# Turning B by DMA, three half blocks first, one tile's statistics on ScalarE, one power for the root in the opening part of a fused layernorm, SSM and SwiGLU kernel

## Chip, cores, metric

One core of a Trainium2 chip. The metric is device time of the whole program in microseconds (us), median of several executions, compared with the kernel before on the same chip. The kernel before takes 190.64 us; its executions lie within 0.2%.

The engines are called as the profile does: PE is TensorE (matmul), PEld its weight loads, DVE VectorE, ACT ScalarE, POOL GpSimd, SP SyncE (here it mainly issues DMAs). A letter q behind a name is the engine's instruction queue. The granted clock is the share of its full clock that TensorE is given. L428 is line 428 of that kernel's source; the numbers shift between kernels.

## The reference, cut to what matters

```python
def _A_ref(x, ...):                       # SSM: x is 2048 tokens x 448
    Lam_bar = exp(exp(log_dt) * Lam)
    Bu = einsum("bld,pd->blp", x, B_bar)  # "bu": needs B turned, as matmul weights
    for t in range(L): h = Lam_bar * h + Bu[:, t]
    return 2.0 * einsum("blp,dp->bld", hseq, C).real + x * Dskip

def _B_ref(x, w_gate, w_up, w_down):      # 448 -> 1792 -> 448
    return (silu(x @ w_gate) * (x @ w_up)) @ w_down

x = A_x; xn = layernorm(x)                # mean, variance, 1/sqrt(v + 1e-5)
return x + A(xn) * silu(B(xn))
```

## The kernel before

The 2048 tokens are worked in four quarters of 512 (four tiles of 128 tokens). For a quarter, gate and up take 14 blocks of 128 columns, two at a time ("pairs" of blocks, four banks a pair, of the eight banks of PSUM, into which TensorE writes). ScalarE evicts them, that is, copies them out of PSUM so that the bank is free (`gs` by Silu, `us` by Copy), and VectorE multiplies four blocks in one instruction. The argument touches these parts (cuts marked by ...).

```python
def bank(name, dtype=F32):            # eight banks, handed out in turn
    return psum.tile([P, 2048 // mybir.dt.size(dtype)], dtype, name=name, tag="bank")
...
def gu(q, bg, budget, hooks={}, begun=None):
    ...
            for i in range(0, n, 2):
                fi = f0 + i
                ...
                    banks = gu_banks()
                    gu_matmuls(q, fi, banks, 0, W)
                for j, (gp_, up_) in enumerate(banks):
                    nc.scalar.activation(gs[:, i + j, :], gp_[:], ACT.Silu)
                    nc.scalar.activation(us[:, i + j, :], up_[:], ACT.Copy)
                for fn in hooks.get(fi // 2, ()):   # hook n runs after pair n
                    fn()
```

The matmuls use half the rows of the array each, two at a time. Where the halves change places, GpSimd passes a notice on to TensorE (`tell`: an empty instruction in GpSimd's stream), and powers run on GpSimd between such notices:

```python
def tell(mm):
    told = nc.gpsimd.nop(nofuse=True)
    ...
def ln_sqrt(n0, n1):  power(sd[:, n0:n1], vep[:, n0:n1], halves[:, 0 : n1 - n0])   # on GpSimd
def ln_rstd(n0, n1):  nc.vector.reciprocal(out=rstd[:, n0:n1], in_=sd[:, n0:n1])
```

The rest of the first quarter's work hangs in the hooks. `table_phase` is four VectorE instructions that make the arguments of a cos/sin table, `table_sin` two ScalarE instructions (ST, CT) that evaluate it; `bu` is the group of B's products:

```python
gu(0, bg, 2.0, {
    0: [*stats(4, 5, 6, 7), *sqrt(1), on(params_in), on(table_phase, 0)],
    1: [*bs(1), on(b_clear), *rstd_of(1), *norms(4, 5, 6, 7), on(table_sin, 0)],
    2: [*transposes(4, 5, 6, 7), on(load_c), on(table_phase, 1), on(table_sin, 1),
        on(bu, 0, (0, 1)), on(table_phase, 2), on(table_sin, 2)],
    3: [on(bu, 0, (2,), "between"), on(table_phase, 3), on(table_sin, 3), on(params_fold)],
    4: [on(params_trig), on(ssm_steps, bg, 0)],
    5: [on(params_out)],
}, begun)
```

In these traces ScalarE and VectorE run their instructions in the order of the program: what is written first on ScalarE runs first there, even where it waits (the 3.21 us of waiting before a table, shown below, hold the evictions behind it).

## Time and profile before

| what | value |
|---|---|
| time | 190.64 us |
| TensorE busy | 97% of 188.8 us |
| first gate/up matmul | 7.22 us |
| first `bu` matmul | 19.38 us |
| first matmul of the down projection | 64.3 us |
| last matmul ends | 184.7 us |

From TensorE's and VectorE's timelines of the kernel before (columns: start us, duration us, engine, line, operation, output<-inputs, shapes, count):

```profile
19.38 3.19 PE L428 MATMUL pb<-xT,BT 64*128 64x512 bf16 x28
```

```profile
10.35 0.62 DVE L230 BATCH_NORM_STATS2 st<-x_all 128x6 f32<-128x448 bf16 x1
```

And what TensorE waited for in the whole run (us in total, times, longest):

```profile
PE warm L176 <- DVE Wd L167: 1.2, 1, 1.2
PE tp L259 <- DVE xn L248: 0.6, 2, 0.4
```

The first `bu` group is 28 matmuls in 3.19 us. VectorE starts the statistics of tiles 4 to 7 at 10.35. TensorE waits for nothing after the first transposes.

### The profile page before, as it was taken

Reading aid. Unit: us, or ns where it says so; the run is one execution under the profiler, and the core shown is the slowest. Engines: PE = TensorE matmul, PEld = TensorE weight load, DVE = VectorE, ACT = ScalarE, POOL = GpSimd, SP = SyncE. Lnnn points to the kernel's source line nnn. Section 1 sums busy time; section 2 is a strip of 40 time slices with the busy share of each in tenths; the row PEclk is TensorE's granted clock in tenths of the full one; section 3 lists DMA queues with packets and bytes.
Section 4 is the critical chain, followed back from the end, with each engine's and each line's share of the span. In section 5 each row is a group of like instructions: output and inputs, shape, how many; then the busy total and the mean of one; then the engine's idle time right before and its main releaser. Section 6 shows DMA issues by size and latency. Waiting matters only on the chain.

```text
span 188.8 us, 3686 instructions
## 1 busy us (share of the span) xinstructions
PE 182.8 (97%) x1465; PEld 92.5 (49%) x1465; DVE 160.0 (85%) x265; ACT 104.0 (55%) x197; POOL 10.9 (6%) x21
## 2 busy tenths in 40 slices
PE   7899999999999999999999999999999999999991
PEld 3575435555555455544444455544444455555550
DVE  4889995999999999989999899789259999888073
ACT  3288599939998862008987722107987542302200
POOL 6423100000110000000020000000000000000000
PEclk9999999999999999999999999999999999999999
DMA  5999999100012100021006000020000000020011
GB/s 160 343 380 384 377 144 203 28 0 2 0 31 56 31 0 0 0 72 32 0 5 103 6 0 3 24 73 0 3 2 0 3 0 0 0 76 24 0 38 61
DMA packets 20977, 12.59 MB, mean 67 GB/s; under 512 B 10976, under 2 KB 19936, under 8 KB 20960
## 3 DMA queue, kind: packets, MB, share of 16 engines
q1 hardware_dynamic: 20288, 12.10, 24.5%
q10 hardware_dynamic: 544, 0.26, 0.5%
q8 instruction: 11, 0.18, 0.4%
q14 instruction: 6, 0.05, 0.1%
q0 software_dynamic: 128, 0.00, 0.0%
HBM read 8.03 MB, written 1.84 MB: 52 GB/s over the span
## 4 chain that ended last, share of the span: by engine, by line
PE 94%; DVE 2%; DMA 1%; ACT 0%; POOL 0%; issue 0%; DVEq 0%
PE gp L428 24%; PE hd L567 23%; PE up L428 21%; PE y L581 11%; PE pb L428 10%; PE pk L453 2%; PE y L585 2%; DMA x_all<-in_A_x_dram 1%; PE tpb L371 1%; DVE st L230 1%; PE tp L259 1%; DVE t L594 0%; DVE ob L596 0%; ACT xT L261 0%; POOL sd L215 0%; DVE xn L248 0%
## 5 line engine op out<-in xcount | busy, mean ns | idle before, releaser
L428 PE MATMUL gp<-xT,Wg 64*128 64x512 bf16 (+1 forms) x406 | 86.2, 369 | 0.1
L428 PE MATMUL up<-xT,Wu 64*128 64x512 bf16 (+1 forms) x406 | 85.9, 369 | 0.0
L428 PEld LDWEIGHTS <-Wg 64*128 64x128 bf16 x406 | 37.1, 94 | 23.8 <-issue 1.6
L428 PEld LDWEIGHTS <-Wu 64*128 64x128 bf16 x406 | 37.3, 94 | 19.4 <-POOLq L410 0.3
L567 PE MATMUL hd<-Wd,Vt 128*128 128x448 bf16 x224 | 43.0, 353 | 0.0
L554 ACT ACTIVATE gs<-gp 128x512 bf16<-128x512 f32 x56 | 35.0, 626 | 10.9 <-PE gp L428 7.4
L555 ACT ACTIVATE us<-up 128x512 bf16<-128x512 f32 x56 | 35.4, 632 | 0.0
L567 PEld LDWEIGHTS <-Vt 128*128 128x128 bf16 x224 | 21.8, 98 | 21.0 <-issue 0.8
L572 ACT ACTIVATE sg<-hd 128x448 bf16<-128x448 f32 x16 | 8.7, 544 | 33.7 <-PE hd L567 33.7
L559 DVE TENSOR_TENSOR Vt<-gs,us 128x2048 bf16<-128x2048 bf16 (+1 forms) x16 | 17.3, 1082 | 6.3 <-ACT us L555 6.3
L428 PE MATMUL pb<-xT,BT 64*128 64x512 bf16 x168 | 19.2, 376 | 0.0
L594 DVE TENSOR_TENSOR t<-y,sg 128x448 f32<-128x448 f32 x16 | 10.0, 623 | 10.6 <-PE y L581 10.2
L466 ACT ACTIVATE bu_re<-pb 128x512 bf16<-128x512 f32 x12 | 7.3, 609 | 20.9 <-PE pb L428 20.9
L581 PE MATMUL y<-C,H_re 128*128 128x448 bf16 x64 | 17.4, 352 | 0.0
L504 DVE TENSOR_TENSOR_SCAN bu_re<-rcol,H_re,ere 128x512 bf16<-128x512 f32 x12 | 15.1, 1269 | 0.0
L585 PE MATMUL y<-Dd,xT 128*128 128x128 bf16 x64 | 13.6, 212 | 0.0
L428 PEld LDWEIGHTS <-BT 64*128 64x128 bf16 x168 | 8.4, 94 | 10.0 <-issue 1.3
L581 PE MATMUL y<-C,H_im 128*128 128x448 bf16 x48 | 11.7, 353 | 0.0
L504 DVE TENSOR_TENSOR_SCAN bu_im<-rcol,H_im,eim 128x512 bf16<-128x512 f32 x9 | 11.3, 1260 | 0.0
L230 DVE BATCH_NORM_STATS2 st<-x_all 128x6 f32<-128x448 bf16 x16 | 9.8, 615 | 1.5 <-DMA x_all<-in_A_x_dram 1.5
L596 DVE TENSOR_TENSOR ob<-t,x_all 128x448 bf16<-128x448 f32 x16 | 10.0, 625 | 0.5
L215 POOL TENSOR_TENSOR sd<-vep,halves 128x1 bf16<-128x1 bf16 (+1 forms) x7 | 5.7, 814 | 77.2 <-PE up L428 41.8
(95 smaller groups left out, 174.4 us busy)
## 6 DMA issues: line engine op xcount, KB each, us to landing
out_dram<-ob SPq DMA_DIRECT2D x16, 112.0 KB, 1.7
Wd<-in_B_w_down_dram SPq DMA_DIRECT2D x1, 1568.0 KB, 11.8
x_all<-in_A_x_dram SPq DMA_DIRECT2D x1, 896.0 KB, 13.7
Wg<-in_B_w_gate_dram SPq DMA_DIRECT2D x1, 768.0 KB, 7.0
Wu<-in_B_w_up_dram SPq DMA_DIRECT2D x1, 768.0 KB, 8.5
x_all<-in_A_x_dram SPq DMA_DIRECT2D x1, 448.0 KB, 5.2
Wg<-in_B_w_gate_dram SPq DMA_DIRECT2D x1, 384.0 KB, 5.1
Wu<-in_B_w_up_dram SPq DMA_DIRECT2D x1, 384.0 KB, 5.5
```

Of the source, the lines that this page charges most:

```text
L230: nc.vector.bn_stats(out=st[:], in_=x_all[:, n, :])
L428: mm = nc.tensor.matmul(banks[n][i][:, c0:c1], lhsT=weights[n][i][h, d, :], rhs=xT[h, d, q * W + c0 : q * W + c1], start=(first and m == 0 ...
L504: nc.vector.tensor_tensor_scan(out=T["b"][c][:, k, :], data0=rcol[:, k : k + 1].to_broadcast([P, W]), data1=T["e"][c][:, k, :], initial=in ...
L554: nc.scalar.activation(gs[:, i + j, :], gp_[:], ACT.Silu)
L555: nc.scalar.activation(us[:, i + j, :], up_[:], ACT.Copy)
L559: nc.vector.tensor_tensor(out=Vt[:, f0 : f0 + n, :], in0=gs[:, 0:n, :], in1=us[:, 0:n, :], op=ALU.mult)
L567: nc.tensor.matmul(hd, lhsT=Vt_of[q][:, fi, j * P : (j + 1) * P], rhs=Wd[:, fi, :], start=(fi == 0), stop=(fi == NF - 1),)
L572: nc.scalar.activation(sg[:], hd, ACT.Silu)
L581: nc.tensor.matmul(y, lhsT=h, rhs=C2[:, n, :], start=(n == 0), stop=(n == NS - 1))
L585: nc.tensor.matmul(y[:, s + c0 : s + P], lhsT=xT[:, n, m * P : (m + 1) * P], rhs=Dd[:, n, c0:P], start=False, stop=False,)
L594: nc.vector.tensor_tensor(out=t[:], in0=y, in1=sg[:], op=ALU.mult)
L596: nc.vector.tensor_tensor(out=ob[:], in0=t[:], in1=x_all[:, m, :], op=ALU.add)
```

## The change

The intent is to take work from a busy TensorE: B comes turned by DMA instead of by 32 TensorE transposes; more of the left token half is worked while the right half is being normalised; the statistics and the root get shorter on VectorE. The core of the diff:

```diff
-    for n in range(2):
-        nc.sync.dma_start(out=x_all[:, n, :], in_=x2d[n * P : (n + 1) * P, :])
-    load_x(2, TQ)
-    load_w(nc.sync, nc.sync, Wg, B_w_gate, 0, C0)
-    load_w(nc.scalar, nc.scalar, Wu, B_w_up, 0, C0)
-    load_nat(0, A_B_re)
+    for n, eng in enumerate((nc.sync, nc.sync, nc.scalar, nc.scalar)):
+        eng.dma_start(out=x_all[:, n, :], in_=x2d[n * P : (n + 1) * P, :])
+    load_gu(0, C0)
+    load_gu(C0, 768)
     load_x(TQ, 2 * TQ)
-    load_gu(C0, 768)
-    load_nat(1, A_B_im)
     load_gu(768, F)
+    load_turned(BT, A_B_re, 0, D)
+    load_turned(BT, A_B_im[KF * P : D, :], D, R)
+    load_turned(BT, A_B_im[0 : KF * P, :], KT * P, KF * P)
 ...
-    halves = ctile([P, TQ], BF16, "halves")
-    nc.gpsimd.memset(halves[:], 0.5)
+    halves = ctile([P, TQ], F32, "halves")
+    nc.gpsimd.memset(halves[:], -0.5)
 ...
+    def ln_stats_act(n):
+        nc.scalar.activation(off[:], x_all[:, n, :], ACT.Copy, accum_out=sums3[:, 0:1])
+        nc.scalar.activation(nmean[:], sums3[:, 0:1], ACT.Copy, scale=-1.0 / D)
+        nc.scalar.activation(
+            off[:], x_all[:, n, :], ACT.Square, bias=nmean[:], accum_out=sums3[:, 1:2]
+        )
 ...
-                    nc.scalar.activation(us[:, i + j, :], up_[:], ACT.Copy)
+                    if begun and fi == 0:
+                        nc.vector.tensor_copy(out=us[:, i + j, :], in_=up_[:])
+                    else:
+                        nc.scalar.activation(us[:, i + j, :], up_[:], ACT.Copy)
 ...
+    first, third = gu_banks(), gu_banks(1)
+    C1 = W // 2
+    gu_matmuls(0, 0, first, (0, C1))
+    gu_matmuls(0, 2, third, (0, C1), between=second_tokens)
 ...
-        1: [*bs(1), on(b_clear), *rstd_of(1), *norms(4, 5, 6, 7), on(table_sin, 0)],
-        2: [*transposes(4, 5, 6, 7), on(load_c), on(table_phase, 1), on(table_sin, 1),
-            on(bu, 0, (0, 1)), on(table_phase, 2), on(table_sin, 2)],
-        3: [on(bu, 0, (2,), "between"), on(table_phase, 3), on(table_sin, 3), on(params_fold)],
-        4: [on(params_trig), on(ssm_steps, bg, 0)],
-        5: [on(params_out)],
+        1: [*norms(4, 5, 6, 7), on(table_sin, 0)],
+        2: [*transposes(4, 5, 6, 7), on(load_rest), on(table_phase, 1), on(table_sin, 1),
+            on(table_phase, 2), on(table_sin, 2)],
+        3: [on(table_phase, 3), on(table_sin, 3), on(params_fold)],
+        4: [on(bu, 0, (0, 1)), on(params_trig), on(b_clear)],
+        5: [on(bu, 0, (2,), "between"), on(params_out), on(ssm_steps, bg, 0)],
```

The title's four parts leave out three edits: the `us` copies of the first pair go to VectorE, the `bu` groups move from after the third and fourth pairs to after the fifth and sixth, and tables 1 and 2 now stand together in one hook with no `bu` group between them. Smaller edits are in the diff too: the parameter transposes come earlier, two loads later, and the second quarter runs more background steps per pair (a budget of 1.2 instead of 0.9).

More of the change, by code (lines that the diff above doesn't have):

```diff
@@ L152, in load_gu, with load_turned @@
         load_w(nc.sync, nc.sync, Wu, B_w_up, c0, c1)
-    def load_nat(i, src):
-        nc.sync.dma_start(
-            out=nat[:, i, 0:KF, :], in_=src[0 : KF * P, :].rearrange("(k p) f -> p k f", p=P)
-        )
-        nc.sync.dma_start(out=nat[:, i, KF, :], in_=src[blk(KF), :])
-    def load_turned(dst, src):
+    def load_turned(dst, src, c0, n):
         for k, cols in ((slice(0, KF), slice(0, KF * P)), (slice(KF, KT), blk(KF))):
-            nc.sync.dma_start(out=dst[:, k, :], in_=src[:, cols], transpose=True)
-    nat = big.tile([P, 2, KT, D], BF16, name="nat", tag="vt")
+            nc.sync.dma_start(out=dst[:, k, c0 : c0 + n], in_=src[:, cols], transpose=True)
     natC = ctile([P, 2, KT, D], BF16, "natC")
@@ L181 @@
     C0 = 256
-    for n in range(2):
-        nc.sync.dma_start(out=x_all[:, n, :], in_=x2d[n * P : (n + 1) * P, :])
-    load_x(2, TQ)
-    load_w(nc.sync, nc.sync, Wg, B_w_gate, 0, C0)
-    load_w(nc.scalar, nc.scalar, Wu, B_w_up, 0, C0)
-    load_nat(0, A_B_re)
+    for n, eng in enumerate((nc.sync, nc.sync, nc.scalar, nc.scalar)):
+        eng.dma_start(out=x_all[:, n, :], in_=x2d[n * P : (n + 1) * P, :])
+    load_gu(0, C0)
+    load_gu(C0, 768)
     load_x(TQ, 2 * TQ)
-    load_gu(C0, 768)
-    load_nat(1, A_B_im)
     load_gu(768, F)
+    load_turned(BT, A_B_re, 0, D)
+    load_turned(BT, A_B_im[KF * P : D, :], D, R)
+    load_turned(BT, A_B_im[0 : KF * P, :], KT * P, KF * P)
+    for r, v in enumerate((A_log_dt, A_Lambda_re, A_Lambda_im, A_Dskip)):
+        nc.gpsimd.dma_start(out=vrow[r : r + 1, :], in_=v.unsqueeze(0))
     nc.gpsimd.affine_select(
@@ L196 @@
     )
-    halves = ctile([P, TQ], BF16, "halves")
-    nc.gpsimd.memset(halves[:], 0.5)
+    halves = ctile([P, TQ], F32, "halves")
+    nc.gpsimd.memset(halves[:], -0.5)
     euler = ctile([P, KT], F32, "euler")
     nc.gpsimd.memset(euler[:], math.e)
-    for r, v in enumerate((A_log_dt, A_Lambda_re, A_Lambda_im, A_Dskip)):
-        nc.gpsimd.dma_start(out=vrow[r : r + 1, :], in_=v.unsqueeze(0))
     def count_tokens():
@@ L223 @@
     mv = ctile([P, NT, nc.vector.BN_AGGR_DIM], F32, "mv")
-    vep = ctile([P, NT], BF16, "vep")
-    sd = ctile([P, NT], BF16, "sd")
+    vep = ctile([P, NT], F32, "vep")
     rstd = ctile([P, NT], F32, "rstd")
@@ L234, in ln_stats, with ln_stats_act_out, ln_root @@
         )
-    def ln_sqrt(n0, n1):
-        power(sd[:, n0:n1], vep[:, n0:n1], halves[:, 0 : n1 - n0])
-    def ln_rstd(n0, n1):
-        nc.vector.reciprocal(out=rstd[:, n0:n1], in_=sd[:, n0:n1])
+    sums3 = ctile([P, 2], F32, "sums3")
+    nmean = ctile([P, 1], F32, "nmean")
+    def ln_stats_act(n):
+        off = work.tile([P, D], BF16, name="off", tag="sg", bufs=TQ)
+        nc.scalar.activation(off[:], x_all[:, n, :], ACT.Copy, accum_out=sums3[:, 0:1])
[3 more added lines that the diff above has]
+        )
+    def ln_stats_act_out(n):
+        for out, in_, m, c in ((mv[:, n, 0:1], nmean[:], -1.0, 0.0),
+                               (vep[:, n : n + 1], sums3[:, 1:2], 1.0 / D, 1e-5)):
+            nc.vector.tensor_scalar(
+                out=out, in0=in_, scalar1=m, scalar2=c, op0=ALU.mult, op1=ALU.add
+            )
+    def ln_root(n0, n1):
+        power(rstd[:, n0:n1], vep[:, n0:n1], halves[:, 0 : n1 - n0])
     def ln_norm(n):
@@ L363, in table_sin @@
         cos_sin(CT[:, k, :], ST[:, k, :], *phase.pop(k), two_pi[:] if k == KF else TWO_PI)
-    def b_transpose(c, d, eng):
-        tp = bank("tpb", BF16).rearrange("p (i w) -> p i w", i=2)
-        for i in range(2):
-            for k in (KF, *range(KF)):
-                c0 = blk(k).start if c == 0 else (k + 1) % KT * P
-                nc.tensor.transpose(
-                    tp[:, i, c0 : c0 + P], nat[:, c, k, blk(d + i)], Id[:]
-                )
-        tp = tp[:, :, c * R : c * R + D]
-        dst = BT[:, d : d + 2, c * D : (c + 1) * D]
-        if eng is nc.scalar:
-            nc.scalar.activation(dst, tp, ACT.Copy)
-        else:
-            nc.vector.tensor_copy(out=dst, in_=tp)
     def b_clear():
@@ L415, in told_of, with sums @@
         tc.add_manual_dep(mm.ins, notice, SYNC, reason="other half")
-    def sums(banks, weights, q, c0, c1, between=None, told=None):
+    def sums(banks, weights, q, *cols, between=None):
         left = []
+        cols = cols * (len(banks) if len(cols) == 1 else 1)
         for share, first in ((0, True), (1, False)):
-            for n in range(len(banks)):
+            for n, (c0, c1) in enumerate(cols):
                 for m in range(4 - share):
@@ L436, in sums @@
                     left.append(tell(mm))
-                    if told:
-                        told()
-                        told = None
             if first:
@@ L460, in bu @@
             whole()
-        sums(pb, pairs, q, 0, W, between=whole if packed == "between" else None)
+        sums(pb, pairs, q, (0, W), between=whole if packed == "between" else None)
         if packed == "last":
@@ L529, with gu_banks, gu_matmuls, gu @@
     GRP = 4
-    def gu_banks():
-        return [[bank("gp"), bank("up")] for _ in range(2)]
-    def gu_matmuls(q, f0, banks, c0, c1, **kw):
-        pairs = [[w[:, :, block(f)] for w in (Wg, Wu)] for f in (f0, f0 + 1)]
-        sums(banks, pairs, q, c0, c1, **kw)
-    def gu(q, bg, budget, hooks={}, begun=None):
+    def gu_banks(n=2):
+        return [[bank("gp"), bank("up")] for _ in range(n)]
+    def gu_matmuls(q, f0, banks, *cols, **kw):
+        pairs = [[w[:, :, block(f0 + n)] for w in (Wg, Wu)] for n in range(len(banks))]
+        sums(banks, pairs, q, *cols, **kw)
+    def gu(q, bg, budget, hooks={}, begun={}):
         Vt = big.tile([P, NF, W], BF16, name="Vt", tag="vt")
@@ L547, in gu @@
                 fi = f0 + i
-                if begun and fi == 0:
-                    banks = begun
+                if fi // 2 in begun:
+                    banks = begun[fi // 2]()
                 else:
                     banks = gu_banks()
-                    gu_matmuls(q, fi, banks, 0, W)
+                    gu_matmuls(q, fi, banks, (0, W))
                 for j, (gp_, up_) in enumerate(banks):
                     nc.scalar.activation(gs[:, i + j, :], gp_[:], ACT.Silu)
-                    nc.scalar.activation(us[:, i + j, :], up_[:], ACT.Copy)
+                    if begun and fi == 0:
+                        nc.vector.tensor_copy(out=us[:, i + j, :], in_=up_[:])
+                    else:
+                        nc.scalar.activation(us[:, i + j, :], up_[:], ACT.Copy)
                 for fn in hooks.get(fi // 2, ()):
@@ L606 @@
         ln_stats(n)
-        ln_sqrt(n, n + 1)
+        ln_root(n, n + 1)
         run_power()
+    ln_stats_act(3)
     count_tokens()
     for n in range(2):
-        ln_rstd(n, n + 1)
         ln_norm(n)
@@ L615, with second_tokens, first_pair, second_pair @@
             warm(1)
-    warm(3)
-    for n in range(2, TQ):
-        ln_stats(n)
-        ln_sqrt(n, n + 1)
-    run_power()
-    begun = gu_banks()
-    gu_matmuls(0, 0, begun, 0, W // 2, told=run_power)
-    for n in range(2, TQ):
-        ln_rstd(n, n + 1)
-        ln_norm(n)
-    nc.scalar.activation(pcol[:], params_row(), ACT.Copy)
-    ln_transpose(2, nc.vector)
-    ln_transpose(3, nc.vector)
-    power(dtv[:], euler[:], pcol[:, 0:KT, 0])
-    for d in range(0, KT, 2):
-        b_transpose(0, d, nc.scalar)
-    gu_matmuls(0, 0, begun, W // 2, W)
-    nc.sync.dma_start(out=Wd[:], in_=B_w_down.rearrange("(ft p) d -> p ft d", p=P))
-    load_x(2 * TQ, NT)
+    nc.scalar.activation(pcol[:], params_row(), ACT.Copy)
+    warm(1)
+    ln_stats_act_out(3)
+    ln_stats(2)
+    ln_root(2, TQ)
+    run_power()
+    power(dtv[:], euler[:], pcol[:, 0:KT, 0])
+    ln_norm(3)
+    ln_norm(2)
+    def second_tokens():
+        ln_transpose(3, nc.scalar)
+        ln_transpose(2, nc.vector)
+    first, third = gu_banks(), gu_banks(1)
+    C1 = W // 2
+    gu_matmuls(0, 0, first, (0, C1))
+    gu_matmuls(0, 2, third, (0, C1), between=second_tokens)
+    def first_pair():
+        gu_matmuls(0, 0, first, (C1, W))
+        return first
+    def second_pair():
+        banks = third + gu_banks(1)
+        gu_matmuls(0, 2, banks, (C1, W), (0, W))
+        return banks
     bu_alloc(0)
@@ L644, in transposes, with root, load_rest @@
         return [on(ln_turn, n) for n in ns]
-    def sqrt(q):
-        return [on(ln_sqrt, q * TQ, (q + 1) * TQ)]
-    def rstd_of(q):
-        return [on(ln_rstd, q * TQ, (q + 1) * TQ)]
-    def bs(c):
-        return [on(b_transpose, c, d, nc.vector if d else nc.scalar) for d in range(0, KT, 2)]
-    def load_c():
-        load_turned(natC[:, 0], A_C_re)
-        load_turned(natC[:, 1], A_C_im)
-    gu(0, bg, 2.0, {
-        0: [*stats(4, 5, 6, 7), *sqrt(1), on(params_in), on(table_phase, 0)],
-        1: [*bs(1), on(b_clear), *rstd_of(1), *norms(4, 5, 6, 7), on(table_sin, 0)],
-        2: [*transposes(4, 5, 6, 7), on(load_c), on(table_phase, 1), on(table_sin, 1),
-            on(bu, 0, (0, 1)), on(table_phase, 2), on(table_sin, 2)],
-        3: [on(bu, 0, (2,), "between"), on(table_phase, 3), on(table_sin, 3), on(params_fold)],
-        4: [on(params_trig), on(ssm_steps, bg, 0)],
-        5: [on(params_out)],
-    }, begun)
-    gu(1, bg, 0.9, {
+    def root(q):
+        return [on(ln_root, q * TQ, (q + 1) * TQ)]
+    def load_rest():
+        load_turned(natC[:, 0], A_C_re, 0, D)
+        load_turned(natC[:, 1], A_C_im, 0, D)
+        load_x(2 * TQ, NT)
+        nc.sync.dma_start(out=Wd[:], in_=B_w_down.rearrange("(ft p) d -> p ft d", p=P))
+    gu(0, bg, 2.0, {
+        0: [*stats(4, 5, 6, 7), *root(1), on(params_in), on(table_phase, 0)],
+        1: [*norms(4, 5, 6, 7), on(table_sin, 0)],
[4 more added lines that the diff above has]
+        5: [on(bu, 0, (2,), "between"), on(params_out), on(ssm_steps, bg, 0)],
+    }, {0: first_pair, 1: second_pair})
+    gu(1, bg, 1.2, {
         1: stats(8, 9),
-        2: [*stats(10, 11), *sqrt(2), on(c_weights, 0)],
-        3: [*rstd_of(2), *norms(8, 9), on(c_weights, 1)],
+        2: [*stats(10, 11), *root(2), on(c_weights, 0)],
+        3: [*norms(8, 9), on(c_weights, 1)],
         4: [*norms(10, 11), *transposes(8, 9), on(c_weights, 2)],
@@ L696 @@
                 0: stats(n, n + 1),
-                1: stats(n + 2, n + 3) + sqrt(q + 3),
-                2: rstd_of(q + 3) + norms(n, n + 1),
+                1: stats(n + 2, n + 3) + root(q + 3),
+                2: norms(n, n + 1),
                 3: norms(n + 2, n + 3) + transposes(n, n + 1),
```

## The prediction

> **What bounds the kernel now.** I read the page first (busy shares, then the chain), then the timeline of each engine between 0 and 45 us, because every edit but the root lies there.
>
> The page of the kernel before:
>
> ```profile
> PE 182.8 (97%) x1465; PEld 92.5 (49%) x1465; DVE 160.0 (85%) x265; ACT 104.0 (55%) x197; POOL 10.9 (6%) x21
> ...
> PE 94%; DVE 2%; DMA 1%; ACT 0%; POOL 0%; issue 0%; DVEq 0%
> ```
>
> TensorE is the bound, without a hole from its first real matmul at 7.22 us to its last at 184.7. So the naive sum is simple: what leaves TensorE's stream is gained. But ScalarE and VectorE must hand PSUM banks back in time, and there the slack is almost nil. The timeline of ScalarE, 22 to 29 us:
>
> ```profile
> 22.86 0.63 ACT L305 ACTIVATE ST<-f 128x512 bf16<-128x512 f32 x1 [1.85 <-DVE f L356]
> 23.58 0.72 ACT L306 ACTIVATE CT<-a,half_pi 128x512 bf16<-128x512 f32 x1
> ...
> 26.64 0.74 ACT L306 ACTIVATE CT<-a,half_pi 128x512 bf16<-128x512 f32 x1
> 27.25 0.61 ACT L554 ACTIVATE gs<-gp 128x512 bf16<-128x512 f32 x1
> 27.73 0.62 ACT L555 ACTIVATE us<-up 128x512 bf16<-128x512 f32 x1
> ```
>
> The sine tables sit in ScalarE's stream between the evictions of gate/up pairs and wait for VectorE's phases (1.85 us at the first line). The fourth pair's eviction starts only at 27.25. And TensorE at that time:
>
> ```profile
> 25.42 1.03 PE L428 MATMUL pb<-xT,BT 64*128 64x512 bf16 x8
> 26.38 1.04 PE L453 MATMUL pk<-xT,BT 128*128 128x512 bf16 x4
> 27.35 0.82 PE L428 MATMUL pb<-xT,BT 64*128 64x512 bf16 x6
> 28.01 0.38 PE L428 MATMUL gp<-xT,Wg 64*128 64x512 bf16 x1
> ```
>
> The pair that starts at 28.01 takes over the bank that `gs` left at 27.86 (its other banks a little later). TensorE gets by with under 0.2 us, and only because the two `bu` groups (3.0 and 2.6 us of matmuls) stand in its stream before that point.
>
> **What the skill says.** (1) "PSUM — Partial Sum Buffer", Specifications: eight banks per partition, 512 FP32 values each. The trace agrees in kind: all outputs are at most 512 wide, and the kernel's pool hands out eight in turn. (2) "TensorE: Matmul & The Clock Gate", Architectural detail: ScalarE and VectorE are strict FIFO. The trace agrees: the eviction above stands behind a table that waits. (3) The same page, Part 1: after at least one idle window of some 3.4 us the array falls to half clock, and it takes a busy window to come back. The trace shows the cold side at the start only: warm-up matmuls took 553 to 581 ns, later 352. (4) "VectorE: DVE Perf Modes", Why PSUM operands drop a tier: fp32 from PSUM goes at 1x. The trace has 623 ns for a 448-wide tensor_tensor from PSUM; I take 0.6 us for the new 512-wide copy.
>
> **The change, part by part.**
>
> *B by DMA.* 32 transposes leave TensorE: two rows of 16, about 1.0 us each, so 2.0 us; three 0.93 us copies leave ScalarE and one 0.62 us leaves VectorE. Six DMA transposes come onto SyncE's queue. C's four took 1.25 to 1.95 us to issue and 3.0 to 4.5 to land. Starting near 9 us, B is down by about 23 us. 896 KB of B go from in front of the last weights, so these land earlier. The use of B moves from after the third pair to after the fifth, so the DMAs themselves should be hidden.
>
> *Root and parameters.* One power (about 0.57 us) replaces power and reciprocal (0.15 us and a handover): 0.2 us sooner per stage in the head. The parameter transposes (0.35 us) go before the first gate/up, into waiting time.
>
> *Third tile's statistics on ScalarE.* Two 448-wide passes and a tiny one, about 1.3 us (estimate from the 0.54 us eviction of that width). They precede the first two xT copies and may cost 0 to 0.3 us, against 0.94 us saved on VectorE. First gate/up at 7.0 to 7.4 us.
>
> *Three half blocks.* Before, 1.64 us of half-width work hid the second token half; now another 0.75 us. The extra `Wu` columns are needed at 8.8 us and come at about 9.2 (estimate: 1.41 MB had landed at 7.9, the next at about 334 GB/s). With transposes and copies the second half starts near 10.6 us, as before, but with 0.75 us more done. First pair complete: 12.1.
>
> So far TensorE is 2.0 + 0.35 + 0.2 = about 2.5 us ahead. The naive answer is 188.2 us.
>
> *What comes back.* The first pair's two `us` copies go to VectorE, and in its program order they stand before the statistics of tiles 4 to 7. VectorE started those at 10.35; now it waits for the first pair and starts at about 13.05 (12.45 + 0.6). From there with the old trace's steps:
> - Statistics and parameters to the first phase: 10.35 to 14.67 before, 4.32 us: phase 0 at 17.37.
> - Phase 0: 2.32, to 19.69. (B's copy, its clearing and the reciprocal, 0.97 us, are gone from here.)
> - Eight norms 2.05, the first product 1.13: phase 1 at 22.87 (before 21.14).
> - Phases 1 and 2, 2.33 and 2.46: the third argument is ready at 27.66 (before 25.93).
>
> On ScalarE, both tables 1 and 2 now precede the fourth pair's eviction. The second CT ends its slot 0.61 us after 27.7, so `gs` runs 28.3 to 28.9 and `us` to 29.4.
>
> On TensorE, five pairs now come in a row. Pair 1 ends at 14.4, pair 2 at 17.45, pair 3 at 20.5. Pair 4 needs pair 2's banks, held by the table-0 wait (CT at 19.8, evictions from 20.4, 0.48 apart): start about 21.5, end 24.5, a loss of 1.0. Then the first `bu` group takes pair 3's banks, free only at 29.4: **4.9 us of idle TensorE**.
>
> From there remains what remained before from 28.01 (156.7 us to 184.7), less one pair (3.0), plus the two `bu` groups (2.9 + 2.6): 159.2. TensorE ends at 29.4 + 159.2 = 188.6 instead of 184.7: **+3.9 us**, 194.6 in all. If the idle stretch trips the half clock, 3.4 us at half speed add up to 1.7; I weigh it at one in three, since 4.9 us contain a whole window of 3.4 in not much under half the cases, and shorter stalls never.
>
> *Later.* The scan starts later: B's products are out at about 40.4, first VectorE steps until 47.3 (before 42.3). The rest to H took 30.0 us before, some 0.8 less now: 76.5, and the output sum comes at about 79. Slack about 2.5 us, as before (72.3 against 75.05). No further loss.
>
> **Rivals.**
> - *The gain stands (188 us).* For: TensorE is 97% busy and loses 2.0 us of work. Needs VectorE's phases 5 us sooner than I have them. Against: before had no slack there, and the order of the streams is fixed by the program.
> - *DMA becomes the bound.* B late: the `bu` group would wait for B, not for ScalarE. For: 16 engines are full until 24 us. Against: B has 6 us to spare by my estimate. It would make 195 or more.
> - *H late for the output sum.* VectorE is 99% busy from 64.5 to 75. Would add up to 2 us; the larger budget (1.2 for 0.9) speaks against.
> - *Half the stall.* If the two copies run earlier or phases overlap better by 2 us: 192.5.
>
> **Range and chances.** Sum 194.6, plus one third of 1.7 is 195.1; I take 195.0. The line of 2% is 194.5, within my error: starts of 0.5 us either way on VectorE shift the result one for one, and the clock can add 1.7. Range 191.8 to 197.3. Faster by over 2%: 0.05 (only if I misread the order). Within 2%: 0.34. Slower: 0.61.
>
> **What would show it.** TensorE idle of 4 to 6 us between 24 and 30, put down to ScalarE (or to `gs`/`us`), before the first `pb`; about 1 us before the fifth pair at about 21. VectorE waiting 1 us or more for the first pair, statistics of tiles 4 to 7 from about 13. ScalarE waiting about 3 us for the first ST and 2 for the second. No `tpb` rows, and B's DMAs landed by 24. Warm-speed matmuls after the gap, or 553 ns ones if the clock fell. The prediction is wrong if `pb` starts before 26, if it waits for a DMA, or if the output sum waits for H.

## More of the kernel before

The runs of the experiments went to two chips (e1 to e4 to one, e5 to e11 to another), on which the kernel before takes 190.66 and 190.77 to 190.83 us, so that totals can be set side by side.

## The result and the profile after

The changed kernel takes 199.19 us (197.89 to 199.38, four executions), the kernel before 190.64: ratio 1.0431, 95% interval 1.0386 to 1.0476. Ratios are the mean time of one kernel's executions over that of the other's of the same rounds, so not quite the ratio of the medians. The direction was predicted; the size is twice that predicted, and 199.2 lies outside the range.

The page of the changed kernel (busy shares; then TensorE's busy tenths and granted clock in 40 slices of 4.9 us; then the chain by engine):

```profile
PE 185.0 (94%) x1445; PEld 91.2 (46%) x1445; DVE 158.9 (81%) x257; ACT 103.3 (52%) x198; POOL 11.3 (6%) x20
...
PE   7798927999999999999999999999999999999991
...
PEclk9999995899999999999999999999999999999999
...
PE 82%; DVE 8%; DMA 4%; issue 2%; ACT 1%; SPq 0%; POOLq 0%; DVEq 0%
```

Two things to see: slice 6 (24.7 to 29.6 us) has TensorE at 2 tenths, and in slice 7 its clock is at 5 tenths. From slice 9 on TensorE is as busy as before; slices 2 and 4 are a little emptier than before (7 and 8 tenths for 8 and 9). From the first to the last down matmul it is 114.4 us against 114.0 before; the first down matmul comes at 72.2 us instead of 64.3. So 7.9 of the 8.5 us were lost before 72.2 us.

What TensorE waited for in the changed kernel:

```profile
PE pb L421 <- ACT gs L544: 4.5, 1, 4.5
PE warm L169 <- DVE Wd L160: 1.2, 1, 1.2
PE up L421 <- POOLq L401: 1.1, 2, 0.9
PE tp L266 <- DVE mv L242: 0.5, 1, 0.5
PE gp L421 <- ACT xT L268: 0.3, 1, 0.3
PE up L421 <- DMA Wu<-in_B_w_up_dram: 0.3, 1, 0.3
```

The `bu` group itself, from TensorE's timeline (in brackets the idle time before it and what ended it):

```profile
30.61 6.08 PE L421 MATMUL pb<-xT,BT 64*128 64x512 bf16 x28 [4.50 <-ACT gs L544]
```

It waits 4.5 us for an eviction, and then its 28 matmuls take 6.08 us where 3.19 were needed. ScalarE's timeline says why the eviction is late:

```profile
20.35 0.63 ACT L312 ACTIVATE ST<-f 128x512 bf16<-128x512 f32 x1 [3.21 <-DVE f L363]
...
25.85 0.63 ACT L312 ACTIVATE ST<-f 128x512 bf16<-128x512 f32 x1 [2.10 <-DVE f L363]
...
28.63 0.63 ACT L312 ACTIVATE ST<-f 128x512 bf16<-128x512 f32 x1 [1.33 <-DVE f L363]
29.36 0.72 ACT L313 ACTIVATE CT<-a,half_pi 128x512 bf16<-128x512 f32 x1
29.98 0.58 ACT L544 ACTIVATE gs<-gp 128x512 bf16<-128x512 f32 x1
```

ScalarE stands still for 6.6 us in all, waiting for VectorE's phases, and for most of that time matmul results that it could evict lie in PSUM. VectorE's phases are late because of this:

```profile
13.12 1.29 DVE L546 CAST us<-up 128x512 bf16<-128x512 f32 x2 [1.47 <-PE gp L421]
14.32 0.62 DVE L221 BATCH_NORM_STATS2 st<-x_all 128x6 f32<-128x448 bf16 x1
```

VectorE waits for the first pair, copies it, and begins the statistics at 14.32 instead of 10.35. The clock, from the table of stretches (columns: stretch, its us; busy us of PE, PEld, DVE, ACT, POOL; then PEclk, DMA share, GB/s):

```profile
28.00:29.00 1.00, 0.00 (x0) 0.00 (x0) 0.97 (x2) 0.37 (x1) 0.00 (x0) 1.00 0.58 116
29.00:30.00 1.00, 0.00 (x0) 0.00 (x0) 0.89 (x3) 0.90 (x3) 0.00 (x0) 0.60 0.91 130
...
35.00:36.00 1.00, 1.00 (x8) 0.42 (x6) 0.00 (x0) 0.20 (x2) 0.00 (x0) 0.50 0.90 193
36.00:37.00 1.00, 1.00 (x12) 0.47 (x10) 0.00 (x0) 1.00 (x3) 0.00 (x0) 0.98 0.57 94
```

TensorE's clock is granted in full until 29.2 us (the 0.60 is a mean: 0.2 us in full, 0.8 us at half) and at half from then to 36.0: 6.8 us, nearly all of the `bu` group.

### The profile page after: what moved, and what is told of

The parts are those of the page before. It is cut to its first block, busy times and chain, and to the rows that moved or that the text cites. A ratio compares the mean times of both kernels' runs of the same rounds, so it can differ in the third digit from the quotient of the medians.

```text
span 197.4 us, 3640 instructions
## 1 busy us (share of the span) xinstructions
PE 185.0 (94%) x1445; PEld 91.2 (46%) x1445; DVE 158.9 (81%) x257; ACT 103.3 (52%) x198; POOL 11.3 (6%) x20
## 4 chain that ended last, share of the span: by engine, by line
PE 82%; DVE 8%; DMA 4%; issue 2%; ACT 1%; SPq 0%; POOLq 0%; DVEq 0%
PE hd L560 22%; PE gp L421 18%; PE up L421 17%; PE pb L421 11%; PE y L574 11%; DMA Wu<-in_B_w_up_dram 2%; PE pk L443 2%; DMA Wg<-in_B_w_gate_dram 2%; PE y L578 2%; DVE st L221 1%; DVE f L363 1%; DVE a L364 1%; DVE xn L255 1%; ACT CT L313 1%; DVE a L360 1%
## 5 line engine op out<-in xcount | busy, mean ns | idle before, releaser
L421 PEld LDWEIGHTS <-Wg 64*128 64x128 bf16 x413 | 37.7, 94 | 23.1 <-issue 0.8
L544 ACT ACTIVATE gs<-gp 128x512 bf16<-128x512 f32 x56 | 33.9, 607 | 13.1 <-PE gp L421 10.4
L548 ACT ACTIVATE us<-up 128x512 bf16<-128x512 f32 x54 | 33.1, 613 | 0.0
L421 PE MATMUL pb<-xT,BT 64*128 64x512 bf16 x168 | 22.6, 412 | 4.5 <-ACT gs L544 4.5
L421 PEld LDWEIGHTS <-BT 64*128 64x128 bf16 x168 | 9.2, 101 | 17.3 <-issue 10.1
L207 POOL TENSOR_TENSOR rstd<-vep,halves 128x4 f32<-128x4 f32 (+2 forms) x6 | 5.9, 980 | 91.6 <-PE up L421 42.2
L221 DVE BATCH_NORM_STATS2 st<-x_all 128x6 f32<-128x448 bf16 x15 | 9.2, 615 | 1.5 <-DMA x_all<-in_A_x_dram 1.5
```

What stands on the lines that cost most here:

```text
L221: nc.vector.bn_stats(out=st[:], in_=x_all[:, n, :])
L421: mm = nc.tensor.matmul(banks[n][i][:, c0:c1], lhsT=weights[n][i][h, d, :], rhs=xT[h, d, q * W + c0 : q * W + c1], start=(first and m == 0 ...
```

## The experiments

Theory A: VectorE's late phases hold the tables, the tables stand before evictions on ScalarE, TensorE waits for the banks, and the idle time trips its clock. Theory B: B's transposing DMAs, or the weights that they disturb, set the pace. All kernels gave correct results. This table sums up (times to the first `bu` matmul and to the first down matmul are from each profile):

| kernel | first `bu`, us | idle before it | its 28 matmuls, us | first down | total, us | ratio to before |
|---|---|---|---|---|---|---|
| before | 19.38 | 0 | 3.19 | 64.3 | 190.64 | 1 |
| changed | 30.61 | 4.50 | 6.08 | 72.2 | 199.19 | 1.0431 |
| e1 | 28.84 | 4.10 | 5.15 | 69.5 | 196.25 | 1.0292 |
| e2 | 31.05 | 0.29 | 3.78 | 70.5 | 197.68 | 1.0362 |
| e3 | 25.75 | 0 | 3.19 | 68.3 | 195.21 | 1.0245 |
| e4 | 19.74 | 0 | 3.19 | 64.5 | 190.66 | 0.9997 |
| e5 | 25.72 | 0 | 3.19 | 64.5 | 191.27 | 1.0028 |
| e6 | 25.02 | 0 | 3.19 | 63.8 | 190.58 | 0.9981 |
| e7 | 26.54 | 2.19 | 5.35 | 67.4 | 193.79 | 1.0156 |
| e8 | 24.14 | 0 | 3.20 | 62.9 | 189.94 | 0.9960 |
| e9 | 24.16 | 0 | 3.30 | 63.1 | 189.63 | 0.9941 |
| e10 | 27.48 | 0 | 3.19 | 66.3 | 192.56 | 1.0082 |
| e11 | 24.42 | 1.41 within it | 3.66 busy | 65.1 | 192.05 | 1.0074 |

From the first `bu` to the first down matmul it is 38.8 us in e5, e6, e8 and e10, and 38.9 in e9: that is the stretch with no wait in it. The changed kernel needs 41.6.

### e1: the first pair's `us` back on ScalarE

```diff
-                    if begun and fi == 0:
-                        nc.vector.tensor_copy(out=us[:, i + j, :], in_=up_[:])
-                    else:
-                        nc.scalar.activation(us[:, i + j, :], up_[:], ACT.Copy)
+                    nc.scalar.activation(us[:, i + j, :], up_[:], ACT.Copy)
```

> The changed kernel with one thing undone: the two us copies of the first pair go back from VectorE to ScalarE, so VectorE need not wait for the first pair (2.7 us) before the statistics of tiles 4 to 7. Theory A (VectorE's late phases hold the sine tables, these stand before the fourth pair's evictions on ScalarE, and TensorE waits for the banks): the first bu matmul starts near 28.0 instead of 30.6; TensorE idle before it falls from 4.5 to about 3 us; 196.5 us if the half clock comes all the same, 193.5 if it does not. Theory B (the transposing DMAs of B or the late weights set the pace): no change, 199 us.

Measured: 196.25 us (195.94 to 196.58). `bu` starts 1.8 us sooner, and the wait before it is still 4.1 us, for TensorE comes sooner as well: its wait for GpSimd's notice fell from 1.1 to 0.2 us in all.

```profile
28.84 5.15 PE L421 MATMUL pb<-xT,BT 64*128 64x512 bf16 x28 [4.10 <-ACT gs L544]
```

This is for A: the total is what A gave for "the half clock comes all the same", with `bu` 0.8 us later than expected. B gave no change. The clock was at half for 3.4 us here, from 28.95.

### e2: useless matmuls in the idle time

```diff
                     banks = gu_banks()
+                    if q == 0 and fi == 8:
+                        for _ in range(20):
+                            for b, w, h in ((banks[0][0], Wg, H1), (banks[0][1], Wu, H2)):
+                                nc.tensor.matmul(b[:], lhsT=w[h, 0, 0:P], rhs=xT[h, 0, 0:W],
+                                                 start=True, stop=True)
                     gu_matmuls(q, fi, banks, (0, W))
```

> The changed kernel with 20 useless pairs of 64-row matmuls (20 x 0.216 = 4.3 us) put before the fifth pair, into banks that its real matmuls overwrite (results stay right). They fill time that TensorE otherwise stands idle before the first bu matmul, and change no order on another engine. Theory A with the clock: the bu group still starts near 30.6, but at full speed, 3.1 us instead of 6.1: total about 196.2 us, 3 us faster with 4.3 us more work. If the slow bu matmuls are slow for another reason than an idle array (late B, a busy memory): 199 us or more, bu still 6 us.

Measured: 197.68 us (196.84 to 198.14), with 4.3 us more work, and no matmul of the `bu` group at half clock (their longest lasted 387 ns, in the changed kernel 631).

```profile
31.05 3.78 PE L421 MATMUL pb<-xT,BT 64*128 64x512 bf16 x28 [0.29 <-ACT gs L549]
```

From the first `bu` to the first down matmul it is 39.5 us instead of 41.6: **2.1 us is what the half clock cost** beyond the wait itself. I had expected 3 us of the total and got 1.5. The other 0.9 us of the 3 were hidden: even at full speed the group runs into ScalarE's backlog (3.78 us instead of 3.19, as the fourth pair's banks come free one by one). And this execution's profile has `bu` 0.4 us later, after 1.0 us of waiting for the third block's `Wu`. ScalarE's evictions are shifted by the same 0.4 us (30.42 for 29.98), so the two stretches can be compared; each is from one profile, and the intervals of the two totals just touch (ratios 1.0330 to 1.0394 and 1.0386 to 1.0476).

### e3: each table behind a later eviction

```diff
-        1: [*norms(4, 5, 6, 7), on(table_sin, 0)],
-        2: [*transposes(4, 5, 6, 7), on(load_rest), on(table_phase, 1), on(table_sin, 1),
-            on(table_phase, 2), on(table_sin, 2)],
-        3: [on(table_phase, 3), on(table_sin, 3), on(params_fold)],
-        4: [on(bu, 0, (0, 1)), on(params_trig), on(b_clear)],
-        5: [on(bu, 0, (2,), "between"), on(params_out), on(ssm_steps, bg, 0)],
+        1: norms(4, 5, 6, 7),
+        2: [*transposes(4, 5, 6, 7), on(load_rest), on(table_sin, 0), on(table_phase, 1)],
+        3: [on(table_sin, 1), on(table_phase, 2), on(params_fold)],
+        4: [on(bu, 0, (0, 1)), on(params_trig), on(table_sin, 2), on(table_phase, 3),
+            on(b_clear)],
+        5: [on(bu, 0, (2,), "between"), on(table_sin, 3), on(params_out),
+            on(ssm_steps, bg, 0)],
```

> The changed kernel with only the sine tables moved: each ScalarE table behind the eviction of the next gate/up pair (tables 0, 1, 2, 3 in the slots after pairs 2, 3, 4 and the second bu, phases 1, 2, 3 one slot later than before), so no eviction waits for VectorE's phases. Theory A: the bu group starts near 25 to 26 us with under 1.5 us of idle time and at full clock: 191 to 192 us. Theory B (B's DMAs or weights): TensorE waits for B instead, and the total stays at 197 or more.

(Tables 0 and 1 move by one slot, 2 and 3 by two. The expectation is not exact on one point: phase 1 stays in its slot, and only phases 2 and 3 move.)

Measured: 195.21 us (195.10 to 195.95). The wait before `bu` is gone and the clock stays whole, as A has it, and B's DMAs did not hold the group. But the total is 3 us worse than expected, partly from my own edit. The clearing of B's padding (`b_clear`) now stood behind the third phase on VectorE, and the packed `bu` product needs it:

```profile
34.72 0.39 PE L443 MATMUL pk<-xT,BT 128*128 128x512 bf16 x1 [1.15 <-DVE lam L342]
```

(The line names the instruction after the memset.) Further on, the last table stood behind the second `bu`'s evictions, VectorE's scan began only at 40.07 us with a product behind it that ScalarE waited 3.8 us for, and TensorE lost another 1.5 us at 46.5 us to a missing bank. A wait removed at one point came back as the same kind of wait further down.

### e4: the root alone, on the kernel before

```diff
-        power(sd[:, n0:n1], vep[:, n0:n1], halves[:, 0 : n1 - n0])      # bf16, 0.5
-        nc.vector.reciprocal(out=rstd[:, n0:n1], in_=sd[:, n0:n1])
+        power(rstd[:, n0:n1], vep[:, n0:n1], halves[:, 0 : n1 - n0])    # fp32, -0.5
```

> The kernel before with one part of the change alone: root as one power of -1/2 in FP32, the reciprocals gone. If the root is innocent: 190.4 us (0.2 us sooner to the first gate/up matmul, 1.1 us less VectorE work off the path), at most 0.3 us either way. A rival that blames the power (longer on GpSimd in FP32, holding back the notices that GpSimd gives TensorE) would show 191 us or more.

Measured: 190.66 us, ratio 0.9997 (0.9982 to 1.0012). The root is innocent and worth nothing either: the second tile's norm starts at 5.62 instead of 5.67 us but lasts 0.61 us instead of 0.41, so that the 0.2 us expected in the head did not come. The first gate/up matmul is at 7.59 us in this profile, later than the 7.22 before. Why the norm is slower is open: GpSimd's iota ran beside it in both kernels.

### e5: both repairs of e1 and e3

On top of e1, the hooks of e3 with `b_clear` first in hook 4 and the last table first in hook 5.

> The changed kernel with both repairs together: us copies of the first pair on ScalarE, each sine table behind the next eviction, and the clearing of B's padding ahead of the third phase (in e3 it made the packed bu matmuls wait 1.1 us). Theory A: no wait of TensorE for evictions before the bu group and no wait for GpSimd's notices; 191.5 us. What is then left over the kernel before is the head: the first matmul 0.5 us later (statistics on ScalarE), 0.3 to 0.7 us for the third block's Wu, 0.4 us for the copies of the second tokens. If the B transposes or the later bu products hold the rest back by themselves: 193 us or more.

Measured: 191.27 us (190.22 to 192.53), ratio 1.0028 (0.9981 to 1.0074), as expected in the median. No wait for evictions, and the stretch to the first down matmul is down to 38.8 us. So ScalarE's order and VectorE's start account for about 8 of the 8.5 us, give or take 1 us. The scatter of this kernel is larger than that of the others, and its cause is open: the profiled execution (191.49 us) has the clock at half from 8.0 to 11.5 us,

```profile
PEclk9879999999999999999999999999999999999999
```

but the slowest (192.53) has a mean clock of 1.0. In the 3.4 us before that fall no wait of TensorE is longer than 0.52 us; it does small transposes there, with gaps between them.

### e6: the statistics on VectorE again

```diff
-    ln_stats_act(3)
 ...
-    ln_stats_act_out(3)
+    ln_stats(3)
     ln_stats(2)
```

> The run before with one more part undone: the third tile's statistics on VectorE again. If the two ScalarE passes (with their accumulator reads) are what delays the first gate/up matmul from 7.2 to 7.7 us: first matmul at 7.2 and 0.4 to 0.5 us less, 191.1 us. If the wait for the third block's Wu (landing near 9.8) swallows it: first matmul at 7.2 all the same, but the total unchanged within 0.2 us.

Measured: 190.58 us (190.16 to 190.79), ratio 0.9981 (0.9965 to 0.9998). In the profiles the first gate/up matmul moves from 7.96 to 7.54 us, and the first `bu` comes 0.7 us sooner, though the wait for the third block's `Wu` is now 1.1 us. Neither shows what the statistics cost. The intervals of e5 and e6 overlap. e5's profile has the half clock in just this stretch, and its second tokens' transposes start 0.7 us later (11.70 for 11.00), which is all of the move of `bu`. And e11, which has these statistics on VectorE too, starts at 7.75 us, like the changed kernel (7.76). The start is 7.54, not the 7.2 that I expected; e4, with the new root alone, starts at 7.59.

### e7: B by DMA alone, on the kernel before

The natural loads, the TensorE transposes and their evictions go, the six transposing DMAs come after the weights, and the hooks (with the reciprocals kept) and the second quarter's budget of 1.2 are those of the changed kernel; nothing else.

> The kernel before with one part of the change alone: B by transposing DMAs and, since it comes later, the bu products after the fifth and sixth pairs; the tables stay where they were (1 and 2 in one slot ahead of the fourth pair's evictions). Theory A says that this part alone already makes TensorE wait, since the bu group no longer stands in its stream while ScalarE waits for the phases: bu starts near 27 instead of after 24.5, 2 to 3 us idle, 192 to 193 us. The naive theory (2.0 us of transposes leave a busy TensorE): 188.7 us.

Measured: 193.79 us (193.11 to 194.45), ratio 1.0156 (1.0120 to 1.0193).

```profile
26.54 5.35 PE L406 MATMUL pb<-xT,BT 64*128 64x512 bf16 x28 [2.19 <-ACT gs L532]
```

A holds: this part alone, which removes 2.0 us of TensorE's work, costs 3 us. The naive 188.7 is far off. Its clock is the surprise (stretches as above):

```profile
25.00:26.00 1.00, 0.00 (x0) 0.00 (x0) 0.89 (x3) 0.90 (x3) 0.00 (x0) 1.00 0.94 304
27.00:28.00 1.00, 0.98 (x8) 0.45 (x9) 0.96 (x4) 1.00 (x3) 0.00 (x0) 0.84 1.09 382
28.00:29.00 1.00, 1.00 (x8) 0.52 (x7) 0.90 (x7) 1.00 (x2) 0.00 (x0) 0.50 1.09 381
30.00:31.00 1.00, 1.00 (x7) 0.38 (x4) 0.43 (x2) 1.00 (x3) 0.00 (x0) 0.50 1.09 380
31.00:32.00 1.00, 1.00 (x12) 0.54 (x10) 0.00 (x0) 0.83 (x3) 0.00 (x0) 0.95 1.26 334
```

After only 2.2 us of idle time the clock halves, and it does so at 27.7, 1.2 us after work has begun again, for 3.4 us. The four executions fall in two groups: 194.42 and 194.45 us at a mean clock of 0.989 and 0.990, and 193.16 and 193.11 us at 0.996 and 0.997. The kernel before, whose profile shows half clock only after the last matmul, has 0.995 to 1.0. So it seems that here the same program tripped the clock in two executions and not in the two others, for 1.3 us.

### e8: e7 with the tables late

The hooks of e5, the rest of e7.

> The run before plus the tables moved behind the next evictions, as in e5; nothing else of the change. Theory A: the wait goes and the transposes' time is gained, less what they had covered of the second tokens' copies: 189 to 190 us, faster than the kernel before by 0.5 to 1 us. If B's landing (near 25 us) holds the bu group: 190.5 to 191.5 us.

Measured: 189.94 us (189.88 to 190.37), ratio 0.9960 (0.9945 to 0.9975): 3.9 us less than e7 by moving eight ScalarE instructions and, on VectorE, two phases and the clearing. Now B by DMA is a gain, of 0.7 to 0.9 us. Part of the 2.0 us of transposes had covered the second tokens' copies, for which TensorE now waits (the waits of TensorE):

```profile
PE gp L406 <- DVE xT L257: 0.6, 1, 0.6
```

### e9: e8 with the root and one copy on ScalarE

```diff
-    ln_transpose(2, nc.vector)
+    ln_transpose(2, nc.scalar)
```

and the root of e4.

> The kernel before with B by transposing DMAs, the bu products after pairs five and six, the tables behind the next evictions (as e8, 189.94 us), and two small things more: the root as one power (0.2 us of the head, if anything reaches the path) and the second tokens' first copy on ScalarE, so that the two copies that e8's TensorE waits 0.6 us for run side by side. Expected 189.4 us (0.3 us from the copies, 0.2 from the root); if the wait only moves to the norms or the transposes, 189.9 as e8.

Measured: 189.63 us (189.44 to 190.05, six executions), ratio 0.9941 (0.9927 to 0.9955). **This is the lowest median**, 1.2 us under the kernel before and 9.6 under the changed one. The wait that I aimed at only fell from 0.6 to 0.5 us; its step of 0.3 us over e8 is between the two outcomes that I had set out. The intervals of e8 and e9 overlap, so that the step is not shown, and which of the two edits it would come from is open.

No run has the three half blocks alone. The nearest comparison is e6 with e9: e6 has them, with their order of loads and the earlier parameter transposes, e9 has not, and e6 is slower (0.9981 for 0.9941, intervals apart). So they brought no gain as they stand; which of these is to blame is not shown.

### e10: the third block's weights first

On top of e6:

```diff
-    load_gu(C0, 768)
+    load_gu(C0, 384)
+    load_gu(384, 768)
     load_x(TQ, 2 * TQ)
```

> e6 (190.58 us: the changed kernel with us on ScalarE, tables late, statistics on VectorE) with the load of columns 256 to 768 cut in two, so that the third block's 128 columns come before the rest. If the 1.1 us that TensorE waits for Wu in e6 is the last piece that eats the gain: the wait gone, 189.5 to 189.8 us. If the four extra DMA issues of SyncE (about 0.5 us each) make the later weights or B late instead: a new wait at the fourth pair or at the bu group, 190.5 us or more.

Measured: 192.56 us (191.51 to 193.27), a miss: 2 us slower than e6. The wait for `Wu` is gone, and in its place stands a new one. Waits of TensorE, then VectorE's and GpSimd's timelines:

```profile
PE up L422 <- POOLq L402: 2.5, 2, 2.2
```

```profile
14.48 0.63 DVE L222 BATCH_NORM_STATS2 st<-x_all 128x6 f32<-128x448 bf16 x1 [4.03 <-DMA x_all<-in_A_x_dram]
```

```profile
18.41 1.01 POOL L208 TENSOR_TENSOR rstd<-vep,halves 128x4 f32<-128x4 f32 x1 [8.63 <-DVE zi L305]
```

Read them backwards. TensorE needs GpSimd's notice that the halves may change places. That notice stands in GpSimd's stream behind the power for tiles 4 to 7. The power waits for VectorE's statistics, and these wait 4.0 us for tiles of x that the extra issues pushed back. None of these instructions has to do with the matmul that waits. In this profile the clock fell too, after those 2.2 us, and stayed at half from 18.9 to 22.3 us:

```profile
PEclk9999699999999999999999999999999999999998
```

By the mean clock (0.987, the others 0.997 to 1.0) this came in two of the six executions, 193.00 and 191.90 us; the slowest (193.27) is not one of them, so the half clock is not what makes e10 slow. The changed kernel has the same wait for 0.9 us, where the long wait for evictions covers it.

### e11: x before those weights

```diff
     load_gu(C0, 384)
+    load_x(TQ, 2 * TQ)
     load_gu(384, 768)
-    load_x(TQ, 2 * TQ)
```

> e10 (192.56 us) with tiles 4 to 7 of x loaded before columns 384 to 768 instead of after them. In e10 VectorE waited 4.0 us for these tiles, GpSimd's power waited for VectorE, and GpSimd's notice to TensorE stood behind that power (2.2 us of TensorE). If that chain is the whole of e10's miss: no wait for GpSimd over 0.3 us, 190.0 us. If the later weights (448 KB further back) become the next wait: a wait for Wu near 12 us and 190.5 to 191 us. If neither moves it: 192.5 us.

Measured: 192.05 us (191.80 to 192.85), again a miss in the total. The wait for GpSimd is down to 0.3 us, so the chain of e10 was right, and `bu` starts at 24.42. But there a third wait comes, the one of theory B:

```profile
PE pb L422 <- DMA BT<-in_A_B_im_dram: 1.4, 1, 1.4
```

B's imaginary part lands only near 26.9 us here. e6 reaches `bu` at 25.02 and has no such wait; e11 issues B's first transpose 1.8 us later than e6 (11.62 for 9.79). So B has hardly any slack: it is the bound when TensorE reaches `bu` at 24.4 and its issue is that much later. The 1.4 us do not account for all of the distance to the 190.0 us expected; what the other 0.6 us are is open.

## Why the prediction was wrong

**Right.** The chain was predicted and is in the trace: `us` copies, late statistics, late phases, tables before evictions, banks, and an idle TensorE before `bu` (4.9 us predicted, 4.5 measured). e3 and e5 show it by removing it. That the two numbers lie so close is partly luck: the group started 1.2 us later than predicted, but TensorE also arrived 1.6 us later (26.1 for 24.5). One predicted link did not come, the 1.0 us of waiting before the fifth pair: TensorE was late there itself, after 0.9 us of waiting for GpSimd's notice, and no bank held it. Also right: the slack that the `bu` groups gave in the kernel before (e7 loses 3 us by moving them), and that from `bu` to the first down matmul 38.8 us remain without other waits (64.3 + 3.9 - 29.4 by the prediction's numbers; e5, e6, e8 and e10 have just that). The output sum did not wait for H. B came down somewhat later than the 23 to 24 us predicted (its last transpose was issued at 22.0 and took at least 2.4 us), and nothing waited for it in the changed kernel.

**The term that was mis-sized: the clock.** The prediction gave the half clock 3.4 us and a chance of one in three, with "shorter stalls never". None of it held. The clock was at half for 6.8 us in the profile, and by its mean it fell in every execution of the changed kernel (0.978 to 0.986, where the kernel before has 0.995 to 1.0; 6.8 us alone bring the mean to 0.983, so the fastest, 197.89 us with 0.986, had less of it). And e7 and e10 show it after an idle stretch of 2.2 us, e5 with no wait over 0.52 us. By e2 the cost is 2.1 us net; the term stood in the sum at about 0.4.

**The start of the chain.** "First pair complete: 12.1" was 13.4, and its first block, for which VectorE's copies wait, came at 13.1. The first gate/up matmul came at 7.76 us (7.0 to 7.4 predicted), since ScalarE's statistics took 1.7 us from 5.04 to 6.74, two accumulator reads included, and stood before the xT copies (that they put off the start is read from the trace; e6 did not confirm it). Then 0.3 us of waiting for `Wu`, and the second tokens' copies ended at 11.6 instead of 10.6. The statistics of tile 4 started 1.3 us later than predicted, and phase 2 lost 0.5 us more to a buffer that table 1 still read. So the fourth pair's first eviction was 1.7 us late (29.98 for 28.3). `bu` came at 30.6 instead of 29.4, only 1.2 us late, because it starts when the first bank is free and not, as the prediction had it, when two are.

**Behind `bu`.** 0.7 us that the prediction had as none: also with the array at full clock (e2) the stretch is 39.5 us and not 38.8, since ScalarE has to work off its evictions first, and the group waits for the other banks after it has started. e2 has 0.6 of it inside the group.

The three terms, 1.2 + 2.1 + 0.7, make 4.0 of the 4.6 us between the prediction's sum, 194.6, and 199.2 (its 195.0 has 0.4 for the clock in it); the remaining 0.6 us are spread over the second half (114.4 against 114.0 us, and the tail).

**What the prediction did not see** is GpSimd's notice. It cost nothing in the changed kernel, where a longer wait covers it, but it decided e10.

## What to carry to other kernels

Work taken off the bounding engine pays only if the next one can hand over as fast: before removing work, look at how long the engine would have to wait for buffers at that place without it. On an engine that runs in program order, put an instruction that waits for another engine behind the evictions that free buffers, not ahead of them (eight ScalarE instructions moved so were worth about 4 us here, twice). And count an idle stretch of the array of more than 2 us as possibly costing another 1 to 2 us of half clock: it did so after 4.5 us (2.1 us, by e2) and, in two of four executions, after 2.2 us (1.3 us, e7). After single waits of 1.1 to 1.5 us (e3, e6, e11) the profiles show no fall; in e5 the clock fell without any such wait.

## What the Trainium skill lacked or had wrong

- "TensorE: Matmul & The Clock Gate", Part 1, and there the advice of no idle gaps above about 3.4 us: e7 and e10 had the clock halved after 2.2 us of idle time, and e5 with no wait over 0.52 us, so the safe gap was shorter than that. (A later passage of the same part does tell of short, frequent idle times that make the clock swing, but gives no length.) The halved stretches, 3.4 us in e1, e5, e7 and e10 and 6.8 us in the changed kernel, agree with one and two of the windows of about 3.4 us that the page gives. Of the 3.4 us just before the fall TensorE was busy for 9% in the changed kernel, 3% in e1, 32% in e7, 35% in e10 and 65% in e5; in e11 a stretch of that length with 73% brought no fall. This speaks for a share of a window and against the length of one gap; a threshold was not measured.
- "DMA: Bandwidth & Descriptors", Latency and other measured facts, gives 261 GB/s for a DMA transpose with non-contiguous middle dimension. No run here tests that figure: in the changed kernel, in the two slices from 19.7 to 29.6 us, when transposes are nearly all that moves, the whole core moves 91 and 101 GB/s, but its DMA engines are busy for only 4 and 7 tenths of that time. What this case adds is how long a transpose holds the issuing queue: B's two first ones took 3.3 and 5.0 us to issue behind the weights, the later ones 1.2 to 1.35 us, and landing took up to 10.1 us.
- None of the pages cited here warns that a notice that is passed on by a third engine inherits whatever that engine's queue waits for: 0.9 us of TensorE in the changed kernel, 2.2 us in e10, behind a power that had nothing to do with it.
